# Batch 0's decay rows by a selecting matmul, and copies to q and k that write neighbouring tokens

## The chip, the cores and the metric

The kernel runs on one core of a Trainium2 chip. The metric is the device time of one execution in microseconds, median of the runs. Five engines work side by side, each through its own list of instructions in a fixed order: TensorE (PE; its weight loads are shown apart as PEld), VectorE (DVE), ScalarE (ACT), GpSimd (POOL) and SyncE (SP, which here only issues DMAs).

## The reference

Forgetting attention (causal, with a decay per token), then a gated feed-forward block over all tokens. Batch 8, 8 heads, 576 tokens, head size 64; 4608 tokens of width 512, inner width 1536; everything is given in float32.

```python
scores = scale * np.matmul(q, k.transpose(0, 1, 3, 2))
log_f = np.log(np.clip(f, 0.0001, 1.0))
cum = np.cumsum(log_f, axis=-1)
decay = cum[:, :, :, None] - cum[:, :, None, :]
scores = np.where(causal, -1000000000.0, scores + decay)
attn = softmax(scores)                      # over the last axis
x = np.matmul(attn, v)                      # heads put side by side: (4608, 512)
g = x @ w_gate
out = (g * sigmoid(g) * (x @ w_val)) @ w_out
```

## The kernel before

**Layout.** Scores are taken with the head's 64 values on the partitions. The tile QK holds, for a pair of heads, q and k turned that way, and below them on partitions 64 to 67 four rows for the decay. On q's side these are the cumulated sum times 8 and three rows of ones; on k's side a row of ones and the sum times -8, split into three bf16 parts (high, middle, low). So one matmul over 68 partitions (L581) gives scores and decay. ACT takes the exponential to PT or PTa (L589), POOL masks the diagonal blocks (L598), PE multiplies by v with a column of ones (L612), DVE divides (L619, L626, L628), PE turns the result (L636), and a copy puts it in xT, from where the feed-forward reads.

**Feed-forward.** Per tile of tokens twelve blocks of the inner width: four matmuls with w_gate and four with w_val (L713), tanh on ACT (L717), two operations on DVE (L721, L725). Then w_out (L729), a copy on ACT (L733) and a store on SP (L736). The first 576 tokens, batch 0, are cut into tiles of 256 and 320.

**How q and k come to QK.** Batches 2 to 7: POOL casts them to a bf16 tensor in DRAM (`narrow`), and SP issues transposing loads from there (L452), with the decay rows from DRAM (L455). Batches 0 and 1 don't go that way. Their q and k are loaded as they lie, several neighbouring tokens to a partition (2 in batch 0's first 256 tokens, 4 in its last 320, 6 in batch 1), cast to bf16 in BF, turned by PE (`turn`, L419) with two of the tokens of a partition, 64 values each, on the 128 output partitions, and copied by ACT or DVE (L296, L298) from PSUM to QK. Since a turn leaves tokens of the same place in their partition side by side, the copies (`straighten`, `straighten_a`, `straighten_b`) read PSUM in order and write every sixth, second or fourth token of QK:

```python
dst = QK[:D, hqk[p].i, x::2, :S].rearrange("p j (c u t) -> p j u c t", u=QT // 2, t=2)[:, :, :, :, u]
src = ps(bt).bitcast(BF16)[u * D : (u + 1) * D, :S].rearrange("p (j u c) -> p j u c", j=2, u=QT // 2)
copy(e, dst, src)
```

**Decay rows.** f is loaded with its 64 heads on partitions 0 to 63 and worked in two parts of the tokens (256, then 320): clip, ln, scan, up, high, rest, middle, low (L341 to L364), into `dec`. SP then issues DMAs that put the rows of batch 0 in QK (`row`, L367: four for the first part, four for the second), those of batch 1 (four more) and those of the other batches in DRAM (L392).

**Order.** The kernel writes its instructions by a plan of its own. Each operation has a cost per engine, the operations that it follows, buffers that it takes and a key; `Plan.run` goes through time by these costs and gives each engine the ready operation with the smallest key. The program's order on each engine is fixed by that. Constants steer it: `ready` times for loads (W_AT, WO_AT, Q1_AT, V1_AT), PACE0 and PACE for the transposing loads of batches 2 to 7, TWARM for the time until which PE is taken at half speed, and up to IDLE_TO PE gets dummy matmuls (L819) where it has nothing. PSUM has eight banks: four in pool "f", two in "s", one in "o", one in "t"; early on other work may take banks of "f" and "s".

The functions that the change touches, and what calls them, with their line numbers:

Of the kernel before, what the change touches and what calls it, by code (L numbers as in the profile page):

```python
# [189 lines left out]
PACE, PACE0 = 8.92, 50.3  # L190
# [3 lines left out]
def kernel(ctx, tc, q, k, v, f, w_gate, w_val, w_out, out):  # L194
# [54 lines left out]
    lf, zero, cum, r1 = [HHA[:BH, 2 * i : 2 * i + 2].rearrange("p a s -> p (a s)").bitcast(F32) for i in range(4)]  # L249
    dec = HHA[:BH, 8:16].rearrange("p (r w) s -> p r w s", w=2)  # L250
# [15 lines left out]
    TWARM = 20.0  # L266
# [41 lines left out]

    def ld_f(e):
        nc.scalar.dma_start(out=lf, in_=f.rearrange("b h s -> (b h) s"))  # L310

    o_f = op(("ACT", 0.5), ld_f, key=-9, dma=0.6)
    o_zero = op(("POOL", 0.5), lambda e: nc.gpsimd.memset(zero, 0.0), key=-9)
    o_id = op(("POOL", 0.8), lambda e: make_identity(nc, ident[:, :]), key=-8)
# [19 lines left out]
    o_dec = [op(("DVE", 0.5), blank, "dec", key=-7), op(("DVE", 1.5), blank, "dec1", key=-7)]  # L334
# [5 lines left out]
    def clip(e, a, z):  # L340
        nc.vector.tensor_scalar(out=lf[:, a:z], in0=lf[:, a:z], scalar1=1e-4, scalar2=1.0, op0=ALU.max, op1=ALU.min)  # L341

    def ln(e, a, z):
        nc.scalar.activation(lf[:, a:z], lf[:, a:z], AF.Ln)

    def scan(e, a, z):
        nc.vector.tensor_tensor_scan(out=cum[:, a:z], data0=lf[:, a:z], data1=zero[:, a:z],
                                     initial=cum[:, a - 1 : a] if a else 0.0, op0=ALU.add, op1=ALU.add)

    def up(e, a, z):  # L350
        nc.scalar.activation(dec[:, 0, 0, a:z], cum[:, a:z], AF.Copy, scale=8.0)

    def high(e, a, z):
        nc.vector.tensor_scalar_mul(dec[:, 1, 1, a:z], cum[:, a:z], -8.0)

    def rest(e, a, z):
        nc.vector.scalar_tensor_tensor(out=r1[:, a:z], in0=cum[:, a:z], scalar=-8.0, in1=dec[:, 1, 1, a:z],
                                       op0=ALU.mult, op1=ALU.subtract)

    def middle(e, a, z):  # L360
        nc.vector.tensor_copy(dec[:, 2, 1, a:z], r1[:, a:z])

    def low(e, a, z):
        nc.vector.tensor_sub(dec[:, 3, 1, a:z], r1[:, a:z], dec[:, 2, 1, a:z])  # L364
# [7 lines left out]
    gates, o_row, prior = [], [], []  # L372
    for k0, a, z in ((-9, 0, HALF), (5, HALF, S)):
        n = z - a
        c = op(("DVE", dve(n, False)), clip, a, z, after=[o_f], key=k0, tag="clip")
        c = op(("ACT", act(n)), ln, a, z, after=[c], key=k0, tag="ln")
        c = op(("DVE", 0.1 + n / 480), scan, a, z, after=[c, o_zero] + prior, key=k0, tag="scan")
        prior = [c]
        u = op(("ACT", act(n)), up, a, z, after=[c], key=k0, tag="up")
        g = op(("DVE", dve(n, False)), high, a, z, after=[c], key=k0, tag="high")  # L380
        x = op(("DVE", dve(n, False)), rest, a, z, after=[g], key=k0, tag="rest")
        m = op(("DVE", dve(n, False)), middle, a, z, after=[x], key=k0, tag="middle")
        x = op(("DVE", dve(n, False)), low, a, z, after=[m], key=k0, tag="low")
        four = ((0, [u, o_dec[0]]), (1, [g, o_dec[1]]), (2, [m, o_dec[1]]), (3, [x, o_dec[1]]))
        o_row.append([op(("SP", SPi), row, r, 0, a, z, after=w, key=k0 if k0 > 0 else -4.5, dma=0.05 + n / 640, pkt=40.0, tag=("row", r))
                      for r, w in four])
        gates += [u, g, m, x]
    o_row1 = [op(("SP", SPi), row, r, 1, 0, S, after=gates + o_dec, key=95, dma=0.9, pkt=60.0, tag=("row1", r)) for r in range(4)]
    o_warm = op(("ACT", 1.4), lambda e: nc.scalar.activation(warm, cum[:1, :1], AF.Exp), after=gates, key=-9)
# [7 lines left out]
    gone = [o_decd] + o_row[0] + o_row[1] + o_row1  # L397
# [18 lines left out]
    def turn(e, bb, bt, m, w, blocks):  # L416
        t = ps(bt).bitcast(BF16)
        for n in range(blocks):
            nc.tensor.transpose(t[:, n * m : n * m + w], BF[bb.i][: P if w == P else m, n * P : (n + 1) * P],  # L419
                                ident if w == P else ident[:m, :w])  # L420

    def straighten(e, p, x, u, bt):
        dst = QK[:D, hqk[p].i, x::2, :S].rearrange("p j (c u t) -> p j u c t", u=QT // 2, t=2)[:, :, :, :, u]
        src = ps(bt).bitcast(BF16)[u * D : (u + 1) * D, :S].rearrange("p (j u c) -> p j u c", j=2, u=QT // 2)
        copy(e, dst, src)

    def pair_of(g, x):
        i = hqk[2 * g].i
        assert hqk[2 * g + 1].i == i + 1
        return QK[:D, i : i + 2].rearrange("p s (j w) t -> p (s j) w t", w=2)[:, :, x]  # L430

    def straighten_a(e, g, x, u, bt):
        dst = pair_of(g, x)[:, :, :HALF].rearrange("p h (c t) -> p h c t", t=2)[:, :, :, u]
        src = ps(bt).bitcast(BF16)[u * D : (u + 1) * D, : 4 * P].rearrange("p (h c) -> p h c", h=4)
        copy(e, dst, src)

    def straighten_b(e, g, x, u, bt):
        dst = pair_of(g, x)[:, :, HALF:S].rearrange("p h (c u t) -> p h u c t", u=TB // 2, t=2)[:, :, :, :, u]
        src = ps(bt).bitcast(BF16)[u * D : (u + 1) * D, : 8 * PB].rearrange("p (h u c) -> p h u c", h=4, u=TB // 2)
        copy(e, dst, src)  # L440
# [53 lines left out]

    def first_queries(g, key_a, key_b):
        ps2 = (2 * g, 2 * g + 1)
        took = []
        for part, kk0, ld, st, m, w, blocks, n, cost in (
            ("a", key_a, ld_a, straighten_a, P, P, 4, 4 * P, {"ACT": 0.55, "DVE": 0.66}),
            ("b", key_b, ld_b, straighten_b, PB, PB, 8, 8 * P, {"ACT": 0.66, "DVE": 0.8}),  # L500
        ):
            ready = []
            for x, nm in enumerate("qk"):
                kk = kk0 + 0.1 * x + 0.2 * g
                bn = Buf("nata") if part == "a" else Buf("natb", "natw")
                bb, bt = Buf("bf"), Buf("t", ("f", 30.0), ("s", 30.0))
                o1 = op(("SP", SPi), ld, g, nm, bn, take=[bn], key=kk, dma=1.2 if part == "a" else 1.4, pkt=40.0 if part == "a" else 70.0,
                        tag=("ld" + part, g, x), ready=0.0 if part == "a" else 6.5)
                o2 = op({"DVE": n / 1700 + 0.12, "ACT": act(n)}, cast_n,
# [3 lines left out]
                o3 = op(("PE", mm(*[P] * blocks)), turn, bb, bt, m, w, blocks, after=[o2, o_id], take=[bt], use=[bb], key=kk,  # L513
                        tag=("turn" + part, g, x))
                for u in range(2):
                    first = not took
                    o4 = op(cost, st, g, x, u, bt, after=[o3] + ([took[0]] if took else []),
                            take=[hqk[p] for p in ps2] if first else [], use=[bt] if first else [bt] + [hqk[p] for p in ps2],
                            key=kk, tag=("str" + part, g, x, u))
                    if first:  # L520
                        took.append(o4)
# [338 lines left out]
```

## Time and profile before

| | |
|---|---|
| median of 3 runs | 460.34 us (457.36 to 464.15) |
| the profiled execution | 460.65 us, its span 458.9 us |
| PE busy | 407.6 us, 89% of the span |
| PE weight loads | 234.5 us, 51% |
| DVE / ACT / POOL busy | 237.9 / 237.8 / 125.6 us |
| moved by DMA | 50.09 MB, 109 GB/s over the span |
| mean granted PE clock | 0.94 |

Busy times are those of instructions on the engine; an engine can be busy and still not be what the end waits for. The chain that ended last is followed back from the last instruction, each step to what released it. In it PE has 74% of the span, DMA 7%, ACT 7%, DVE 5%, and the issuing on SP 4%. Lines are those of the kernel before.

### The profile page before, as it was taken

How to read it: one execution, taken by the hardware profiler on the slowest of the kernel's cores; microseconds unless marked ns; L12 is line 12 of the kernel's file. 1: busy time of each engine (PE TensorE's matmuls, PEld its weight loads, DVE VectorE, ACT ScalarE, POOL GpSimd, SP SyncE). 2: the span in 40 equal slices, each digit the busy share in tenths (PEclk: the TensorE clock that was granted, in tenths of full speed). 3: DMA queues.
4: the chain of work that ended last, by engine and by line, in shares of the span. 5: the costliest groups of instructions: out<-in, count | busy, mean ns of one | idle time of the engine just before them, and what ended most of it. 6: DMA issues, size and time to landing. Idle time of an engine off the chain costs nothing.

```text
span 458.9 us, 8374 instructions
## 1 busy us (share of the span) xinstructions
PE 407.6 (89%) x3121; PEld 234.5 (51%) x3121; DVE 237.9 (52%) x438; ACT 237.8 (52%) x445; POOL 125.6 (27%) x353
## 2 busy tenths in 40 slices
PE   5769379777999389999979999799999999999996
PEld 3556357544455146655545565356654444444542
DVE  6583557544376114775245735563477184382660
ACT  3858666774357247764755565356662332332331
POOL 9457216013115116434333243223320000000000
PEclk9978759898999869999997999989999999999999
DMA  9999990009777968599799587964400200101102
GB/s 186 191 160 239 200 219 9 0 25 176 129 153 133 75 137 213 109 183 141 174 193 142 88 124 103 206 107 102 87 1 2 91 1 24 69 1 46 47 0 81
DMA packets 112648, 50.09 MB, mean 109 GB/s; under 512 B 97312, under 2 KB 107360, under 8 KB 112224
## 3 DMA queue, kind: packets, MB, share of 16 engines
q1 hardware_dynamic: 97824, 36.44, 40.3%
q0 software_dynamic: 14704, 12.98, 21.1%
q8 instruction: 24, 0.39, 0.4%
q10 hardware_dynamic: 80, 0.15, 0.1%
q14 instruction: 16, 0.13, 0.1%
HBM read 38.34 MB, written 16.96 MB: 120 GB/s over the span
## 4 chain that ended last, share of the span: by engine, by line
PE 74%; DMA 7%; ACT 7%; DVE 5%; SPq 4%; issue 1%; POOL 0%; ACTq 0%; DVEq 0%
PE ps L713 35%; PE ps L729 20%; PE ps L581 9%; PE ps L612 6%; ACT QK L296 5%; DVE QK L298 3%; DMA natv<-in_v_dram 3%; SPq L452 3%; DMA QK<-dec_d 2%; PE ps L636 2%; PE ps L419 1%; DMA QK<-hh 1%; DMA hh<-in_f_dram 1%; ACT PT L589 1%; SPq L461 1%
## 5 line engine op out<-in xcount | busy, mean ns | idle before, releaser
L713 PE MATMUL ps<-xT,wv 128*128 128x512 bf16 (+3 forms) x480 | 117.0, 368 | 1.6 <-DVE QK L298 1.6
L713 PE MATMUL ps<-xT,wg 128*128 128x512 bf16 (+3 forms) x480 | 116.9, 367 | 0.0
L589 ACT ACTIVATE PT<-ps 128x512 bf16<-128x512 f32 (+2 forms) x192 | 91.8, 518 | 43.6 <-PE ps L581 35.1
L721 DVE SCALAR_TENSOR_TENSOR th<-th,ps 128x512 f32<-128x512 f32 (+3 forms) x120 | 75.7, 631 | 68.7 <-ACT th L717 68.3
L729 PE MATMUL ps<-wo,hh 128*128 128x512 bf16 (+1 forms) x444 | 108.3, 385 | 0.0
L717 ACT ACTIVATE th<-ps 128x512 f32<-128x512 f32 (+3 forms) x120 | 67.1, 561 | 76.7 <-PE ps L713 74.5
L581 PE MATMUL ps<-QK 68*128 68x320 bf16 (+4 forms) x448 | 78.4, 277 | 17.0 <-DMA QK<-dec_d 13.2
L725 DVE TENSOR_TENSOR hh<-th,ps 128x512 bf16<-128x512 f32 (+3 forms) x120 | 76.1, 634 | 15.0 <-PE ps L713 3.8
L598 POOL TENSOR_SCALAR_AFFINE_SELECT PT<-PT 128x128 bf16<-128x128 bf16 (+1 forms) x192 | 52.2, 274 | 107.0 <-ACT PT L589 101.3
L713 PEld LDWEIGHTS <-wv 128*128 128x128 bf16 x480 | 47.2, 100 | 41.2 <-issue 2.9
L713 PEld LDWEIGHTS <-wg 128*128 128x128 bf16 x480 | 47.0, 101 | 40.5 <-issue 1.7
L729 PEld LDWEIGHTS <-hh 128*128 128x128 bf16 (+1 forms) x444 | 42.5, 100 | 42.6 <-issue 2.5
L581 PEld LDWEIGHTS <-QK 68*128 68x128 bf16 x448 | 38.2, 103 | 35.3 <-DMA QK<-dec_d 9.9
L619 DVE RECIPROCAL rc<-ps 128x5 f32<-128x5 f32 (+2 forms) x64 | 12.3, 193 | 79.8 <-PE ps L612 79.6
L598 POOL TENSOR_SCALAR_AFFINE_SELECT PTa<-PTa 128x256 bf16<-128x256 bf16 x64 | 26.1, 412 | 92.6 <-ACT PTa L589 90.7
L612 PE MATMUL ps<-VB,PT 128*128 128x65 bf16 x768 | 45.5, 198 | 3.6 <-POOL PT L598 3.6
L733 ACT ACTIVATE ot<-ps 128x512 f32<-128x512 f32 (+1 forms) x37 | 22.1, 597 | 49.4 <-PE ps L729 48.3
L589 ACT ACTIVATE PTa<-ps 128x384 bf16<-128x384 f32 x64 | 30.8, 493 | 28.7 <-PE ps L581 28.4
L612 PEld LDWEIGHTS <-PT 128*128 128x128 bf16 x768 | 37.9, 101 | 14.5 <-POOL PT L598 4.9
L296 ACT ACTIVATE QK<-ps 64x576 bf16<-64x576 bf16 (+2 forms) x19 | 31.4, 1652 | 12.4 <-PE ps L419 9.1
L298 DVE COPY QK<-ps 64x640 bf16<-64x640 bf16 (+2 forms) x13 | 20.4, 1570 | 17.4 <-ACT QK L296 16.6
L626 DVE TENSOR_TENSOR xn<-ps,rc 128x320 bf16<-128x320 f32 x56 | 27.5, 491 | 1.9
(48 smaller groups left out, 190.2 us busy)
## 6 DMA issues: line engine op xcount, KB each, us to landing
out_dram<-ot SPq DMA_DIRECT2D x35, 256.0 KB
natv<-in_v_dram SPq DMA_DIRECT2D x24, 256.0 KB
qk_d<-in_q_dram POOLq DMA_DIRECT2D x6, 576.0 KB, 7.6
qk_d<-in_k_dram POOLq DMA_DIRECT2D x6, 576.0 KB, 11.1
wg<-in_moe_w_gate_dram POOLq DMA_DIRECT2D x3, 512.0 KB, 6.8
wv<-in_moe_w_val_dram POOLq DMA_DIRECT2D x3, 512.0 KB, 10.2
wo<-in_moe_w_out_dram POOLq DMA_DIRECT2D x3, 512.0 KB, 22.9
QK<-qk_d SPq DMA_TRANSPOSE x96
```

Source lines behind the costliest of these rows:

```text
L296: nc.scalar.activation(dst, src, AF.Copy)
L298: E[e].tensor_copy(dst, src)
L581: nc.tensor.matmul(s[:, c : c + w], QK[:KR, hqk[p].i, 2 * j + 1, kt * P : (kt + 1) * P], QK[:KR, hqk[p].i, 2 * j, q0 : q0 + w], start=True ...
L589: nc.scalar.activation(place(h, i)[:, OFFS[i] : OFFS[i] + c], ps(bs)[:, :c], AF.Exp, scale=0.125)
L598: nc.gpsimd.affine_select(out=d, in_=d, pattern=pat, compare_op=ALU.is_ge, fill=0.0, base=0, channel_multiplier=-1,)
L612: nc.tensor.matmul(o[:, lo : lo + D + 1], pt[:, c : c + P], VB[hvb[b].i][:, kt, hb, : D + 1], start=first and n == 0, stop=last and n == l ...
L626: nc.vector.tensor_mul(XN[bx.i][:, qb : qb + nq, j], o, r)
L713: nc.tensor.matmul(ps(bf)[:, :n], w[:, ko, fc * P : (fc + 1) * P], xT[:, ko, t0 : t0 + n], start=(ko == 0), stop=(ko == KD - 1))
L717: nc.scalar.activation(TH[bt.i][:, :n], ps(bf)[:, :n], AF.Tanh, scale=0.5)
L721: nc.vector.scalar_tensor_tensor(out=t, in0=t, scalar=1.0, in1=ps(bf)[:, :n], op0=ALU.add, op1=ALU.mult)
L725: nc.vector.tensor_mul(HH[bh.i][:, lo : lo + n], TH[bt.i][:, :n], ps(bf)[:, :n])
L729: nc.tensor.matmul(ps(bf)[:m, :DM], HH[hs[fc].i][:, lo : lo + m], wo[:, fc, :], start=(fc == 0), stop=(fc == KF - 1))
```

## The change

It has two parts, and the constants of the plan are changed with them.

**Batch 0.** The turn is done head by head (`turn1`, in place of `turn`). The values of one head in BF are the stationary side and the identity the moving side of an ordinary matmul, so the result is float32. Ahead of it a matmul with the selector `sel` writes the whole block of 68 partitions: from 32 prepared rows (`zrow`; four kinds for each of batch 0's eight heads) it picks the head's four onto partitions 64 to 67. One copy (`straighten1`) then takes values and decay rows to QK, for q and k together in the first 256 tokens, one by one in the last 320. It writes neighbouring tokens and reads PSUM in steps. The eight DMAs of `row` for batch 0 go. To prepare `zrow`, batch 0's f is loaded once more, repeated over partitions 0 to 63, and f of all heads now lies on partitions 64 to 127; clip and ln run on both, the scan and five DVE operations (`part0` to `part4`, with masks from POOL as scalars) on the 32 rows in two parts of the tokens. The old chain (scan, up, high, rest, middle, low) runs later, over all tokens at once, for batches 1 to 7.

**Batch 1.** The cast puts the tokens of one head side by side in BF (`cast_t`), so that the turn has the two heads on its output partitions, and the copy of one head (`straighten`) writes neighbours and reads PSUM in steps of 96 elements. There are still sixteen copies of 64x576.

The core of the diff:

```diff
-PACE, PACE0 = 8.92, 50.3
+PACE, PACE0 = 8.64, 54.1
-    TWARM = 20.0
+    TWARM = 3.0
...
+    def ld_f0(e):
+        src = f.rearrange("b h s -> (b h) s")
+        nc.scalar.dma_start(out=lf[: P - BH], in_=src[:H].unsqueeze(0).to_broadcast([(P - BH) // H, H, S]))
     def ld_f(e):
-        nc.scalar.dma_start(out=lf, in_=f.rearrange("b h s -> (b h) s"))
+        nc.scalar.dma_start(out=lf[HI], in_=f.rearrange("b h s -> (b h) s"))
...
+    def selector(e):
+        nc.gpsimd.memset(sel, 0.0)
+        nc.gpsimd.affine_select(
+            out=sel, in_=sel, pattern=[[-1, H], [-H, KR]], compare_op=ALU.not_equal, fill=1.0,
+            base=H * D, channel_multiplier=1,
+        )
...
+    def part0(e, a, z):
+        nc.vector.tensor_scalar(out=zrow[0][:, a:z], in0=cum[LOW, a:z], scalar1=MS[:, 0:1], scalar2=MS[:, 1:2],
+                                op0=ALU.mult, op1=ALU.add)
... (part1 to part4 likewise)
-        o_row.append([op(("SP", SPi), row, r, 0, a, z, after=w, key=k0 if k0 > 0 else -4.5, dma=0.05 + n / 640, pkt=40.0, tag=("row", r))
-                      for r, w in four])
...
+    def cast_t(e, src, bb):
+        copy(e, BF[bb.i][:QP, : QT * P].rearrange("p (t h d) -> p h t d", h=2, d=D), src().rearrange("p h (t d) -> p h t d", d=D))
...
-    def straighten(e, p, x, u, bt):
-        dst = QK[:D, hqk[p].i, x::2, :S].rearrange("p j (c u t) -> p j u c t", u=QT // 2, t=2)[:, :, :, :, u]
-        src = ps(bt).bitcast(BF16)[u * D : (u + 1) * D, :S].rearrange("p (j u c) -> p j u c", j=2, u=QT // 2)
+    def straighten(e, p, x, a, bt):
+        dst = QK[:D, hqk[p].i, 2 * a + x, :S].rearrange("p (c n) -> p c n", n=QT)
+        src = ps(bt).bitcast(BF16)[a * D : (a + 1) * D, :S].rearrange("p (n c) -> p c n", n=QT)
         copy(e, dst, src)
...
+    def turn1(e, h4, xs, bbs, bt, m, nt, lo, h):
+        t, w = ps(bt), m * nt
+        for i, x in enumerate(xs):
+            nc.tensor.matmul(t[:KR, i * w : (i + 1) * w], sel[:, h], zrow[x][:, lo : lo + w].rearrange("p (c t) -> p t c", t=nt),
+                             start=True, stop=True)
+            for n in range(nt):
+                nc.tensor.matmul(t[:D, i * w + n * m : i * w + (n + 1) * m],
+                                 BF[bbs[i].i][:m, (h4 * nt + n) * D : (h4 * nt + n + 1) * D], ident[:m, :m], start=True, stop=True)
+
+    def straighten1(e, h, xs, bt, m, nt, lo):
+        w, j = m * nt, h % 2
+        dst = QK[:KR, hqk[h // 2].i, 2 * j + xs[0] : 2 * j + xs[-1] + 1, lo : lo + w].rearrange("p x (c t) -> p x c t", t=nt)
+        src = ps(bt)[:KR, : len(xs) * w].rearrange("p (x t c) -> p x c t", x=len(xs), t=nt)
         copy(e, dst, src)
...
-    for p in range(FB):
-        attention(p, (100 * p, 1000 + 100 * p), PARTS[0])
+    for p in range(FB):
+        attention(p, (1.2 + 0.6 * p, 1000 + 100 * p), PARTS[0])
...
-W_AT = [0.0, 18.9, 19.0]
-WO_AT = [18.1, 19.0, 22.1]
+W_AT = [0, 9.7, 22.2]
+WO_AT = [26.9, 28.3, 32.3]
-V1_AT = 0.9
+V1_AT = 0
```

In the order that follows from it, SP issues batch 0's eight loads first; then, behind the chain of the other batches' rows, the rows of batch 1, the rows for DRAM, six loads of batch 1, five of v, and the last two of batch 1. The first transposing load stands behind two stores; before, it stood behind one.

## The prediction

> **What bounds the kernel now.** I read the forty slices first, then the chain that ended last, then the groups by shape, then the queue that feeds it.
>
> ```profile
> PE   5769379777999389999979999799999999999996
> DMA  9999990009777968599799587964400200101102
> ```
>
> One digit is 11.5 us. TensorE (PE) is short of full work mainly in the first nine slices. DMA is full for six slices, then rests for three (69 to 103 us), though 24 pairs of heads still have to be fetched. That rest is the odd thing in this profile.
>
> ```profile
> 58.66 2.10 DVE QK L298
> 60.80 0.81 PE ps L419 x6
> 61.63 2.09 ACT QK L296
> 63.75 2.08 DVE QK L298
> 65.87 0.48 PE ps L636 x3
> ```
>
> This is the chain of waits (start, length, what). One copy from PSUM to QK follows the other, on ACT or DVE, with a turn of six matmuls between. PE waits for them: one PSUM bank ("t") holds all these turns.
>
> ```profile
> L296 ACT ACTIVATE QK<-ps 64x576 bf16<-64x576 bf16 x11 | 23.0, 2086 | 6.5 <-PE ps L419 5.6 <-PE ps L612 0.6
> L298 DVE COPY QK<-ps 64x576 bf16<-64x576 bf16 x5 | 10.4, 2074 | 12.5 <-ACT QK L296 12.5
> L298 DVE COPY QK<-ps 64x640 bf16<-64x640 bf16 x5 | 7.9, 1579 | 4.5 <-ACT QK L296 4.1 <-PE ps L419 0.3
> L296 ACT ACTIVATE QK<-ps 64x512 bf16<-64x512 bf16 x5 | 3.7, 735 | 2.7 <-DVE QK L298 2.4 <-PE ps L419 0.3
> L298 DVE COPY xT<-ps 128x576 bf16<-128x576 bf16 x28 | 12.7, 454 | 16.8 <-PE ps L636 16.8
> ```
>
> Groups by shape (busy, mean ns | idle before). The 576-wide copy to QK takes 2.08 us on either engine, the 576-wide copy to xT 0.45. All of them read PSUM in unbroken runs; they differ in where they write. `straighten_a` writes every second token (4 bytes apart): 735/512 = 1.4 ns per element. `straighten_b` writes every fourth (8 bytes): 1585/640 = 2.5. `straighten` writes every sixth (12 bytes): 2080/576 = 3.6. The xT copy writes neighbours: 0.8. Two engines of different speed take the same time, so the write limits them.
>
> ```profile
> 55.80 1.28 SPq L405 DMA_DIRECT2D xT<-in_q_dram  x1
> 57.18 0.82 SPq L405 DMA_DIRECT2D xT<-in_k_dram  x1
> 101.31 0.37 SPq L736 DMA_DIRECT2D out_dram<-ot  x1
> 101.78 3.88 SPq L452 DMA_TRANSPOSE QK<-qk_d  x3
> ```
>
> The timeline of SP's queue: after batch 1's last load its next instruction is the first store, which waits until 101.3 for the first output tile. Every transposing load of batches 2 to 7 stands behind that store. So the time of the first output tile sets when the long middle starts.
>
> ```profile
> 46.60:69.00 22.40, 12.79 (x102) 9.46 (x100) 12.81 (x19) 14.43 (x17) 4.87 (x13) 0.62 1.29 210
> 69.00:101.30 32.30, 26.68 (x228) 18.92 (x226) 20.17 (x42) 23.31 (x37) 8.27 (x20) 0.95 0.01 3
> 101.30:131.50 30.20, 27.65 (x221) 14.93 (x220) 14.35 (x27) 12.41 (x22) 5.21 (x15) 0.94 0.78 147
> 345.00:458.90 113.90, 109.53 (x523) 50.78 (x521) 55.79 (x85) 33.37 (x57) 0.00 (x0) 1.00 0.10 36
> ```
>
> Stretches (length; busy PE, PEld, DVE, ACT, POOL; clock; DMA). From 46.6 to 69 PE is busy 12.8 of 22.4 us, at a granted clock of 0.62. The last 114 us are feed-forward alone, PE full: nothing there changes, it only moves.
>
> **The change, part by part.** All sums are against the profiled execution, 460.65 us (span 458.9 and 1.75 around it); the median of the runs is 460.34, so nothing has to be rescaled.
>
> (1) *Batch 1's sixteen copies.* They now write neighbours and read PSUM in steps of 192 bytes. What such a read costs no row shows. Low end: the engines' own pace. ACT's exponentials of 384 and 512 columns take 487 and 603 ns, 0.91 ns per element, so 576 cost 0.66; DVE's L626 reads 320 floats in 0.49 and L628 reads 384 in 0.56, 1.05 ns each, so 0.76. High end: the strided write read backwards. Cost grew 1.1 ns per 4 bytes of step, so from 16 bytes on 4.7 ns per element, 2.7 us a copy. The one strided read in the trace, L619's reciprocals of 4, 5 and 6 elements 260 bytes apart (178, 194, 193 ns), is too short to decide: two more elements cost 15 ns. I take 0.70. The write side, which made the difference between four shapes, becomes that of the xT row, and that row is nearest in width and place. Fourteen of the sixteen lie on the chain (46.64, 48.74, 51.40, 53.59, 56.54, 58.66, 61.63, 63.75, 86.40, 89.06, 91.18, 98.57, 101.66, 103.67): 14 x (2.08 - 0.70) = 19.3 us. The cover below holds: from 46.6 to the first output copy at 100.7, 54 us, PE has 29 us of matmuls at its full pace (four of 256 columns 0.434, of 320 0.544, of 512 0.86), and ACT and DVE, less their copies, about 17 and 27. So PE becomes the bound there, with room for 19 us.
>
> [...]
>
> (2) *PE's clock.* Between 56 and 69 us and around 91 a group of four 256-column matmuls takes 0.85 us instead of 0.434, after waits of 3.4 to 3.7 us for copies. About 12 such groups lose 5 us; with waits under 1.5 us I count half, 2.5.
>
> (3) *Batch 0, first halves.* Eight copies of 64x512 become eight of 68x2x256 floats, one per head for q and k (0.58 to 0.66 at engine pace). The eight row DMAs of L367, on the chain from 10.88 to 16.1, go. In their place: f again, spread over 64 partitions, for 32 rows; five DVE operations instead of four (0.3 to 0.5 each, 0.92 beside POOL's memsets); per head two matmuls of `sel` and four turning ones, 1024 columns, 0.85 us at the half pace that PE shows until 30 us, so 6.8 for eight heads. All heads' turns stand before the first score. The decay rows are ready at about 9.4 (f lands at 4.84 as before, the logarithm's table of 1.28 us is loaded meanwhile, clip, scan and five parts follow), so the first score starts at about 16, or 13 with PE at full pace, against 16.1. I count nothing, bounds -3 to +3. POOL makes masks and selector first: some 13 small instructions of 0.1 to 0.3, so the first v and weight loads go out about 2 us later; the copies of part (4) hide it.
>
> (4) *Batch 0, second halves.* Eight copies of 1.59 become sixteen of 68x320 (0.38 to 0.46). SP no longer sits in the rows from 13.7 to 26.0, so these loads go out at 3 us instead of 11.6. Before, the copies were done at 34 and the 24 exponentials ended at 46.2; ACT was their bound. In the new order ACT has, from about 16: eight exponentials of 0.49, thirteen copies, five of xT, 24 exponentials (12.4), the moved `up` (0.6) and tanh: about 28 us, so 44. Gain 2, bounds -4 to +5. The chain for the other batches' rows (scan, high, rest, middle, low, now 576 wide, some 4.2 us of DVE) moves behind the first attention. Behind `low` wait on SP the row stores and all loads of batch 1; in the order they come six at once, where before the fifth went out at 45.6 only.
>
> (5) *Extra PE work* (some 50 more matmuls) is 3 us at full pace, in stretches where PE waits anyway; without that cover it costs 3.
>
> Sum: 19.3 + 2.5 + 0 + 2 = 23.8 us. First output copy at about 78 instead of 100.7, the middle and the tail moved by as much: 460.65 - 23.8 = 436.9.
>
> **What is late next.** The first transposing load, on SP, now behind the second store and not the first; and batch 2's v and q, k, for which PE already waits between 131 and 163.
>
> **The rivals.**
>
> *A. The gain is halved by the read.* If the strided read costs what a write 8 bytes apart costs (2.48 ns): 14 x (2.08 - 1.43) = 9; batch 0's copies, 9216 elements over two engines, 11.4 us instead of 9.3, so -2; clock and order 3: 450.6. For it: every broken run in this trace costs something. Against: the rows vary only on the write side.
>
> *B. The queues eat it.* DMA is full until 69, so if batch 1's loads, now behind row stores and `low`, come 8 us later, and the first transposing load waits another 8 for the second store (in the old run the second store went 9.2 us after the first), the middle starts at 78 + 16 = 94 instead of 101.8: 452.8. For it: the middle's waits are for v, rows and transposes. Against: the same bytes were through at 69, nine before I need the queue.
>
> *C. Slower: the read costs more than the write did.* At 4.7 ns per element batch 1's copies take 2.7 us, 14 x 0.62 = 8.7 more; batch 0's 24 copies take 21.7 us per engine instead of 9.3, 12.4 more; 2 come back: 480. The point from which it decides: 14 copies of 0.576 us and 4.6 us of batch 0 make 12.7 us for each ns per element, so from the 24 us won at about 1.2 ns nothing is left at 3.1 ns.
>
> **Numbers.** Forecast 0.60, its own range 428 to 448 (part 2 by 2.5 either way, part 3 by 3, part 4 from -3 to +6 against what I took); A 0.14, B 0.14, C 0.12. The range 425 to 457 leaves out C and a little below. Two per cent, about what a measurement of this kernel can tell from no change, is 9.2 us: faster means below 451.1. All of the forecast, half of A and a quarter of B are there: 0.71. The rest of A and B, within two per cent: 0.17. C: 0.12.
>
> **What would show it.** Right: 64x576 copies to QK of 0.6 to 0.8 us; PE waits under 1.5 us between 45 and 78; the first store near 78; DMA's rest shorter than 15 us; the last stretch of 114 us as it is. Wrong: copies above 1.4 us (A or C), or short copies and a first transposing load after 90 (B); first scores after 19 us would break part 3.

## The result, and the profile after

| | before | after |
|---|---|---|
| median | 462.25 us (457.36 to 464.46, 4 runs) | 441.83 us (440.21 to 445.77, 4 runs) |
| the profiled execution (span) | 460.65 us (458.9) | 440.21 us (438.5) |
| mean granted PE clock | 0.94 | 0.93 |
| first scores | 16.1 us | 22.9 us |
| first store | 101.3 us | 90.0 us |
| from the first store to the end of the span | 357.6 us | 348.5 us |

The ratio is 0.9605, with a 95% interval of 0.948 to 0.973. The change is faster by about 4%, as forecast, and the time is 4.9 us above the forecast of 436.9. Medians are over all runs of a kernel, ratios over undisturbed ones only, so a ratio isn't exactly the quotient of two medians.

The forty slices after, one digit for 11 us:

```profile
PE   4899999999789599999988999999999999999995
...
PEclk8555599999999979999996999999999999999999
DMA  8939899239896988797797679646101101102002
```

PE is now nearly full from the second slice on. But from the second to the fifth slice, 11 to 55 us, its clock is at half. "Busy" and "fast" have come apart: the digits of PE look better than before in just the stretch where the kernel now loses time. DMA's rest, three slices before, is now two slices at two and three tenths, and there is a new slice of three tenths from 22 to 33 us.

The groups by shape, the copies to QK (busy, mean ns | idle before, and what ended it):

```profile
L302 ACT ACTIVATE QK<-ps 64x576 bf16<-64x576 bf16 x10 | 6.4, 644 | 2.8 <-PE ps L475 2.2 <-DVE QK L304 0.6
L304 DVE COPY QK<-ps 64x576 bf16<-64x576 bf16 x6 | 4.5, 758 | 0.8 <-PE ps L475 0.7
L302 ACT ACTIVATE QK<-ps 68x320 bf16<-68x320 f32 x12 | 5.2, 430 | 5.9 <-PE ps L488 5.8
```

Batch 1's copies went from 2.08 us to 0.64 on ACT and 0.76 on DVE, and they hardly wait for each other any more: what ends most of their waits is the turn.

The windows of 9.5 to 23 us, 23 to 57 us, 57 to 90 us and the last stretch (length; busy PE, PEld, DVE, ACT, POOL; clock; DMA):

```profile
9.50:23.00 13.50, 11.26 (x49) 4.92 (x49) 9.49 (x17) 5.11 (x9) 3.08 (x17) 0.50 1.28 168
23.00:57.00 34.00, 34.00 (x261) 22.54 (x261) 12.35 (x29) 21.22 (x52) 18.98 (x47) 0.51 0.89 140
57.00:90.00 33.00, 32.93 (x316) 25.59 (x315) 26.20 (x57) 23.36 (x55) 17.17 (x37) 1.00 0.87 153
325.00:438.50 113.50, 108.36 (x507) 50.21 (x513) 55.14 (x84) 32.98 (x57) 0.00 (x0) 1.00 0.10 37
```

In the second row PE is busy for 34.00 of 34 us at a clock of 0.51. In the third it is as busy, at 1.00. Batch 0's second halves are bound by a PE at half pace; batch 1 is bound by PE at full pace; the tail is as it was.

PE's timeline at the start of batch 0 (start, length, what, idle time before it and what ended it):

```profile
9.48 0.37 PE L485 MATMUL ps<-hh 32*68 32x256 bf16 x1 [3.34 <-DVE hh L381]
...
12.44 0.37 PE L485 MATMUL ps<-hh 32*68 32x256 bf16 x1 [2.24 <-DVE hh L396]
...
13.09 0.42 PE L485 MATMUL ps<-hh 32*68 32x256 bf16 x1
13.44 0.42 PE L488 MATMUL ps<-ident,BF 128*64 128x128 bf16 x2
...
22.90 0.82 PE L644 MATMUL ps<-QK 68*128 68x256 bf16 x4
```

L485 is the selecting matmul (32 rows by 68 columns of the array, 256 moving columns), L488 the two turning ones (128 rows by 64 columns, 128 moving each). Each step of 256 moving columns takes 0.35 us, start to start. The first scores begin at 22.9.

The end of the stretch at half pace:

```profile
44.46 0.48 PE L488 MATMUL ps<-ident,BF 80*64 80x80 bf16 x4
...
52.95 1.04 PE L776 MATMUL ps<-xT,wg 128*128 128x256 bf16 x4
...
56.73 0.60 PE L776 MATMUL ps<-xT,wv 128*128 128x256 bf16 x4
```

The last turn of batch 0 starts at 44.5. Behind it come score, value and gate matmuls and turns of the result, in the shapes of the kernel before, and they too run at half pace until 56.2 (four gate matmuls take 0.84 us, start to start, at 53.0, and 0.44 at 56.7); PE isn't idle in between.

SP's queue:

```profile
42.43 3.24 SPq L416 DMA_DIRECT2D QK<-hh  x4
...
89.96 4.10 SPq L799 DMA_DIRECT2D out_dram<-ot  x2
94.16 5.75 SPq L507 DMA_TRANSPOSE QK<-qk_d  x4
```

The row stores, and batch 1's loads behind them, go out from 42.4 on; the last of the loads is issued by 77.6, so SP rests for 12 us. The first store moved by 11.3 us, the first transposing load by 7.6.

### The profile page after: what moved, and what is told of

It is laid out like the page before. It is cut to its first block, busy times and chain, and to the rows that moved or that the text cites. A ratio compares the mean times of both kernels' runs of the same rounds, so it can differ in the third digit from the quotient of the medians.

```text
span 438.5 us, 8459 instructions
## 1 busy us (share of the span) xinstructions
PE 412.1 (94%) x3127; PEld 237.2 (54%) x3173; DVE 230.2 (52%) x440; ACT 221.6 (51%) x458; POOL 128.4 (29%) x366
## 3 DMA queue, kind: packets, MB, share of 16 engines
q0 software_dynamic: 14704, 12.98, 20.9%
## 4 chain that ended last, share of the span: by engine, by line
PE 89%; DMA 6%; DVE 1%; issue 1%; SPq 1%; ACT 0%; POOL 0%; ACTq 0%; DVEq 0%
PE ps L776 40%; PE ps L792 22%; PE ps L644 11%; PE ps L675 7%; DMA natv<-in_v_dram 4%; PE ps L488 3%; PE ps L485 3%; PE ps L699 2%; DMA hh<-in_f_dram 1%; DMA QK<-dec_d 1%; PE ps L475 1%; SPq L507 0%; ACTq L317 0%; POOL VB L304 0%; DVE hh L385 0%
## 5 line engine op out<-in xcount | busy, mean ns | idle before, releaser
L776 PE MATMUL ps<-xT,wg 128*128 128x512 bf16 (+3 forms) x467 | 112.3, 361 | 0.7
L776 PE MATMUL ps<-xT,wv 128*128 128x512 bf16 (+3 forms) x466 | 111.8, 360 | 0.6
L792 PE MATMUL ps<-wo,hh 128*128 128x512 bf16 (+1 forms) x425 | 104.7, 384 | 1.0
L644 PE MATMUL ps<-QK 68*128 68x320 bf16 (+4 forms) x448 | 79.3, 281 | 7.8 <-DMA QK<-dec_d 7.7
L776 PEld LDWEIGHTS <-wv 128*128 128x128 bf16 x480 | 46.1, 98 | 38.5 <-issue 0.9
L776 PEld LDWEIGHTS <-wg 128*128 128x128 bf16 x480 | 45.5, 98 | 37.8 <-issue 0.5
L792 PEld LDWEIGHTS <-hh 128*128 128x128 bf16 (+1 forms) x444 | 42.0, 99 | 41.4 <-issue 1.9
L675 PE MATMUL ps<-VB,PT 128*128 128x65 bf16 x768 | 47.7, 200 | 4.0 <-POOL PT L661 4.0
L675 PEld LDWEIGHTS <-PT 128*128 128x128 bf16 x768 | 40.1, 102 | 16.9 <-POOL PT L661 4.9
L304 DVE COPY xT<-ps 128x576 bf16<-128x576 bf16 (+1 forms) x30 | 13.4, 445 | 21.0 <-PE ps L699 20.9
L302 ACT ACTIVATE QK<-ps 68x320 bf16<-68x320 f32 (+2 forms) x27 | 14.4, 539 | 13.3 <-PE ps L488 10.4
## 6 DMA issues: line engine op xcount, KB each, us to landing
wo<-in_moe_w_out_dram POOLq DMA_DIRECT2D x3, 512.0 KB, 11.3
```

Source lines behind the costliest of these rows:

```text
L302: nc.scalar.activation(dst, src, AF.Copy)
L644: nc.tensor.matmul(s[:, c : c + w], QK[:KR, hqk[p].i, 2 * j + 1, kt * P : (kt + 1) * P], QK[:KR, hqk[p].i, 2 * j, q0 : q0 + w], start=True ...
L675: nc.tensor.matmul(o[:, lo : lo + D + 1], pt[:, c : c + P], VB[hvb[b].i][:, kt, hb, : D + 1], start=first and n == 0, stop=last and n == l ...
L776: nc.tensor.matmul(ps(bf)[:, :n], w[:, ko, fc * P : (fc + 1) * P], xT[:, ko, t0 : t0 + n], start=(ko == 0), stop=(ko == KD - 1))
L792: nc.tensor.matmul(ps(bf)[:m, :DM], HH[hs[fc].i][:, lo : lo + m], wo[:, fc, :], start=(fc == 0), stop=(fc == KF - 1))
```

## The experiments

Two things had to be explained: what made the 20 us, and why the first store is 12 us later than forecast though the copies came out about as priced (batch 0's on ACT at 0.59 and 0.43 us, on DVE at 0.68 and 0.49). The first theory was that batch 1's copies alone make the gain, and that batch 0's new part costs some of it. The rival was that the gain is in the new order of loads and in the constants of the plan. Ratios are to the kernel before on the same chip.

**Batch 1's part alone.** The kernel before, with `cast_t` and the copies that write neighbours, and the constants and the order of before:

```diff
-        dst = QK[:D, hqk[p].i, x::2, :S].rearrange("p j (c u t) -> p j u c t", u=QT // 2, t=2)[:, :, :, :, u]
...
+        dst = QK[:D, hqk[p].i, 2 * a + x, :S].rearrange("p (c n) -> p c n", n=QT)
...
```

> The kernel before with batch 1's part alone: cast_t and the copies that write neighbours. Constants, costs and so the order of every engine are those of before. Theory 1 (batch 1's copies made the gain, and batch 0's part gave some of it back, since its second half ended later than before): 14 copies on the chain x 1.4 us and some of PE's clock, so 20 to 28 us off, 432 to 441 us, faster than the whole change or level with it; first store near 80. Theory 2 (the new order in the middle made about half of the gain): 448 to 454 us. In both the copies take 0.64 us on ACT and 0.76 on DVE.

Measured: 434.9 us, ratio 0.950 (0.942 to 0.959). Its queue and its windows:

```profile
80.37 0.37 SPq L739 DMA_DIRECT2D out_dram<-ot  x1
```

```profile
9.50:23.00 13.50, 8.91 (x67) 6.40 (x64) 7.75 (x13) 9.89 (x17) 6.92 (x15) 1.00 1.35 189
23.00:57.00 34.00, 26.52 (x305) 20.86 (x306) 23.16 (x49) 24.42 (x52) 20.75 (x50) 1.00 1.24 198
```

The first store is at 80.4, 20.9 us earlier than before. In the two windows PE is less busy than in the changed kernel, and in the second it gets through more matmuls (305 records against 261). So this half of the change alone gives as much as the whole, if not more.

The clock of 1.00 in these rows isn't the pace of the first 31 us. Two lines of the same trace show it:

```profile
8.05 1.92 PE L822 MATMUL ps<-ident 128*128 128x256 bf16 x8
...
31.52 0.60 PE L716 MATMUL ps<-xT,wg 128*128 128x256 bf16 x4
```

Eight dummies of 256 columns take 1.92 us, as at half pace; in the run without a selector, below, sixteen take 1.91. From 31.5 on four matmuls of 256 columns take 0.44, start to start. The kernel before, too, reads 1.00 until 24 us, while its dummies up to 21 us come every 0.21 us. So up to the first scores the half pace of the changed kernel is nothing new; what is new is that it lasts without a break to 56 us.

**Batch 1's part undone.** The changed kernel with all of batch 0's part, its order and constants, and batch 1's cast and copies as before (the diff above backwards).

> The changed kernel with batch 1's cast and copies as before (strided writes of 2.08 us); constants, costs and order are those of the change. Theory 1: sixteen copies 1.4 us longer, of which about twelve end up on the chain: 16 to 22 us lost, 456 to 463 us, no better than before. Theory 2: 446 to 452 us, since the copies lie beside full PE work in the new order.

Measured: 458.8 us, ratio 0.999 (0.994 to 1.005).

```profile
L302 ACT ACTIVATE QK<-ps 64x576 bf16<-64x576 bf16 x10 | 20.9, 2090 | 8.0 <-PE ps L475 6.2 <-DVE rc L682 1.8
```

The copies are back at 2.09 us, and nothing of the gain is left. In the profiled execution, of 461.8 us, the first store is at 104.0.

**The constants alone.**

```diff
-PACE, PACE0 = 8.92, 50.3
+PACE, PACE0 = 8.64, 54.1
...
-W_AT = [0.0, 18.9, 19.0]
-WO_AT = [18.1, 19.0, 22.1]
+W_AT = [0, 9.7, 22.2]
+WO_AT = [26.9, 28.3, 32.3]
...
-V1_AT = 0.9
+V1_AT = 0
```

> The kernel before with the change's constants alone (PACE, PACE0, W_AT, WO_AT, V1_AT), nothing else. Theory 1: the copies are still slow, the first store still near 100: 455 to 467 us, within what the order makes of it. Theory 2: 450 to 456 us, by fewer waits of PE for rows of the decay and v after 110 us.

Measured: 464.2 us, ratio 1.012 (0.999 to 1.025). There is no gain in them. With the two runs above, the rival is out: the write stride of sixteen copies made the gain.

**Batch 0's two waits filled.** PE falls to half pace with the waits of 3.34 and 2.24 us (its clock is 0.95 over the first 9.5 us, and 0.50 from there to 23). Dummies ahead of head 0's selecting matmuls take the waits away. In this kernel they overwrite head 0's q in the first 256 tokens, which is lost.

```diff
+            for _ in range((34, 22)[x] if m == P and h == 0 else 0):
+                nc.tensor.matmul(t[:, :HALF], ident, ident.unsqueeze(1).to_broadcast([P, 2, P]), start=True, stop=True)
```

> The changed kernel with 34 dummy matmuls of 256 columns ahead of head 0's first selecting matmul for q and 22 ahead of the one for k, in which PE waits for the decay rows (3.3 and 2.2 us). If PE's half pace from 9.5 to 57 us comes from these two waits and, once released, full pace is held by the small matmuls, batch 0's stage of 47 us loses 8 to 15 us and the kernel is at 426 to 434 us. If the small matmuls (32 to 80 rows, 64 to 68 columns of the array) do not hold it, the stage is the same length, the granted clock there still 0.5, and the time 438 to 444 us.

Measured: 435.1 us, ratio 0.953 (0.944 to 0.963). PE kept full pace until 18.3 us (a clock of 1.00 from 9.5 to 18), and then lost it without any wait; it was at half until about 49 (0.50 from 23 to 45). The first scores came at 21.5, the first store at 85.7. So in the changed kernel the waits start the half pace, but without them it comes all the same, 9 us later: something else ends the full pace too, and keeps it from coming back.

**The change, and batch 1's part alone, once more on one chip**, to have their distance from each other. Neither has an edit.

> The changed kernel as it is, to stand beside the next three on the same chip: 0.955 to 0.965 of the kernel before.

> Batch 1's part alone, as in the first experiment. If batch 0's part and the new constants give time back, this kernel is faster than the changed one on the same chip: a ratio of 0.945 to 0.955 against 0.955 to 0.965. If the difference of the first experiment was scatter between chips, the two are level within 0.5%.

Measured: the change 440.0 us (433.5 to 443.5), ratio 0.954 (0.944 to 0.964), first store 87.4; batch 1's part alone 432.4 us (430.9 to 436.8), ratio 0.946 (0.940 to 0.951), first store 80.8. Batch 0's new part, with its order and constants, costs 6.6 us in the first store. In the time the two ratios are 0.008 apart, some 4 us; the first run of this part and the result, on two chips, are 0.010 apart. Both point the same way, but the intervals overlap, so a loss in time is likely and not shown.

**A matmul over the whole array in every few.** The waits filled, and ahead of each further selecting matmul of batch 0 one dummy of 256 columns over 128 by 128. That makes one matmul in four in the first halves and one in six in the second.

```diff
+            for _ in range((34, 22)[x] if m == P and h == 0 else 1):
+                nc.tensor.matmul(t[:, i * w : i * w + HALF], ident, ident.unsqueeze(1).to_broadcast([P, 2, P]), start=True, stop=True)
```

> The changed kernel with the two waits of PE filled by dummies (34 and 22) and one dummy matmul of 256 columns over the full 128 x 128 array ahead of every head's selecting matmul, 31 more, 3.3 us of PE work at full pace. If PE is held at half pace because the small matmuls use too little of the array, and a full one in five is enough, the clock from 12 to 50 us is 1.0, batch 0's stage ends near 45 instead of 53, and the time is 428 to 434 us. If a full matmul in five is not enough, the clock stays at 0.5, the dummies cost 6.6 us at half pace, and the time is 443 to 448 us.

Measured: 444.2 us, ratio 0.973 (0.967 to 0.979). Full pace was lost at 18.9 us all the same (a clock of 0.50 from 23 to 45), and the dummies had to be paid for.

**Neighbours without the selecting matmul.** The kernel before with batch 1's part, and the same idea in batch 0's second halves: the cast puts two heads side by side, the old turn over 128 columns stays, and the copies of 64x640 write neighbours. The first halves and the row DMAs are as before.

```diff
-        dst = pair_of(g, x)[:, :, HALF:S].rearrange("p h (c u t) -> p h u c t", u=TB // 2, t=2)[:, :, :, :, u]
...
+        dst = QK[:D, i : i + 2, 2 * u + x, HALF:S].rearrange("p s (c t) -> p s c t", t=TB)
...
+    def cast_b(e, src, bb, m, n):
+        for s in range(2):
+            copy(e, BF[bb.i][:m, s * n // 2 : (s + 1) * n // 2].rearrange("p (t u d) -> p u t d", u=2, d=D),
+                 src()[:, 2 * s : 2 * s + 2].rearrange("p u (t d) -> p u t d", d=D))
```

> The kernel before with batch 1's part, and in batch 0's second half the same without the selecting matmul: the old turn over 128 columns, the rows still by DMA, but the cast sets two heads side by side (two instructions instead of one) and the eight copies of 64x640 write neighbours, 0.7 us instead of 1.59. Six of the eight lay on the chain between 19 and 34 us: 6 x 0.85 less 0.3 for the casts, about 4 us below batch 1's part alone, 428 to 434 us, if exponentials on ACT follow at once. If DMA, which is full until 69 us, or ACT's 24 exponentials hold the stage, level with batch 1's part alone.

Measured: 430.0 us, ratio 0.933 (0.925 to 0.940), first store 76.3 in the profiled execution, of 433.3 us.

```profile
L298 DVE COPY QK<-ps 64x640 bf16<-64x640 bf16 x5 | 4.1, 825 | 2.5 <-ACT QK L296 2.2 <-PE ps L422 0.3
L296 ACT ACTIVATE QK<-ps 64x640 bf16<-64x640 bf16 x3 | 2.1, 697 | 2.5 <-PE ps L422 2.5
```

Copies that took 1.58 us take 0.70 and 0.83. Of the kernels that compute all of the reference this one has the lowest ratio, and its interval lies below that of the change on the same chip.

**Wide turns, and their control.** Is it the 64 columns of the turn that lose the clock? The waits are filled, and each turning matmul takes 128 columns; its second half falls on batch 0's decay rows, which are lost. The control is the run with the waits filled once more, on the same chip.

```diff
...
-                                 BF[bbs[i].i][:m, (h4 * nt + n) * D : (h4 * nt + n + 1) * D], ident[:m, :m], start=True, stop=True)
+                                 BF[bbs[i].i][:m, c : c + P], ident[:m, :m], start=True, stop=True)
```

> The changed kernel with the two waits filled by dummies (as in the run with the gaps filled) and with batch 0's turning matmuls widened: each takes two neighbouring blocks of 64 columns of BF as its stationary side, so that it fills 128 columns of the array instead of 64. The number of matmuls, their moving columns and the copies stay. The second block lands on output partitions 64 to 127, over the decay rows of batch 0, so these are left out of the scores (and the last block of each group of four heads is the one before it). If PE stays at half pace in this stage because the small matmuls fill too few columns: the granted clock from 18 to 45 us is 1.0 or near it instead of 0.62, the turns of batch 0's second halves take 0.4 us per head and tensor instead of 0.8, the gates start at about 44 instead of 50.4, and the time is about 428. If the number of columns doesn't decide (short matmuls, or too few rows, or the gaps between them): full pace is lost at 18 to 19 us as before, and the time is 433 to 440.

> The run with the gaps filled once more, on the same chip as the run with wide turns, as its control (the same edit: head 0's q of the first 256 tokens is lost). If nothing but the width differs between them, this one shows full pace until about 18 us, half pace until about 49, the first store at 85 to 87, and 433 to 440 us.

Measured: wide 437.6 us, ratio 0.959 (0.947 to 0.970); control 434.9 us, ratio 0.953 (0.941 to 0.964). The width of the turn alone changes neither the clock nor, as far as these intervals tell, the time. The window of 18 to 23 us, first with wide turns, then the control:

```profile
18.00:23.00 5.00, 5.00 (x27) 2.57 (x27) 2.94 (x5) 2.29 (x5) 0.22 (x1) 0.50 0.83 95
```

```profile
18.00:23.00 5.00, 5.00 (x24) 2.35 (x25) 2.94 (x5) 1.67 (x3) 0.00 (x0) 0.50 1.01 125
```

While the control still has its full clock, its timeline shows something that the clock doesn't account for:

```profile
14.01 0.30 PE L487 MATMUL ps<-hh 32*68 32x256 bf16 x1
14.24 0.30 PE L490 MATMUL ps<-ident,BF 128*64 128x128 bf16 x2
14.47 0.30 PE L487 MATMUL ps<-hh 32*68 32x256 bf16 x1
```

A step of 256 moving columns takes 0.23 us, start to start. In the feed-forward at full pace four matmuls of 256 take 0.434, so one step should be 0.11.

**No selector.** Wide turns, and a matmul over the whole array in place of each selecting one, with as many moving columns. Batch 0's decay rows are not written at all.

```diff
-            nc.tensor.matmul(t[:KR, i * w : (i + 1) * w], sel[:, h], zrow[x][:, lo : lo + w].rearrange("p (c t) -> p t c", t=nt),
...
+            nc.tensor.matmul(t[:, i * w : i * w + HALF], ident, ident.unsqueeze(1).to_broadcast([P, 2, P]), start=True, stop=True)
...
```

> The run with wide turns, and in place of each selecting matmul (32 rows on 68 columns of the array, 256 or 320 moving columns) a matmul of the identity with itself over the whole array of 128 by 128, with as many moving columns (two instructions, 256 and 64, in the second halves). So batch 0's decay rows aren't written at all; the copies, casts and the order stay. If PE falls back to half pace because the array is filled too little on the average (the selector fills an eighth of it for half of the time): the clock stays 1.0 from 9.5 to 23 us, the first scores start at about 19 instead of 21.7, the stage to 45 us is at 0.8 or more, and the time is 425 to 430. If full pace is lost at 17 to 18 us all the same, the filling of the array isn't the cause, and the time is 433 to 440.

Measured: 426.2 us, ratio 0.929 (0.914 to 0.943). The timeline and the windows, from an execution of 428.5 us:

```profile
14.06 0.27 PE L487 MATMUL ps<-ident 128*128 128x256 bf16 x1
14.17 0.28 PE L492 MATMUL ps<-ident,BF 128*128 128x128 bf16 x2
14.29 0.27 PE L487 MATMUL ps<-ident 128*128 128x256 bf16 x1
```

```profile
18.00:23.00 5.00, 4.23 (x68) 3.41 (x67) 4.30 (x11) 4.78 (x14) 4.26 (x7) 1.00 1.37 143
18.00:45.00 27.00, 24.48 (x318) 20.02 (x317) 17.09 (x39) 21.66 (x56) 23.20 (x50) 0.81 1.13 181
```

In the first window both losses are gone at once: a step takes 0.11 us, and the clock is 1.00. The first scores begin at 17.3. So in this stretch the selector's shape is what costs, not the number of matmuls or columns.

But over the 27 us of the second window the clock is only 0.81. All turns are done, and still:

```profile
31.01 0.59 PE L679 MATMUL ps<-VB,PT 128*128 128x65 bf16 x7 [0.79 <-POOL PT L665]
```

From here to about 41 us PE works at half pace, on score and value matmuls, and it comes out of it when the gates run one after the other (four gate matmuls take 0.84 us, start to start, at 38.4, and 0.44 at 41.4). From 28 to 32 us PE was busy for 2.34 of 4 us, and no single wait was longer than 0.79. So half pace also comes, and stays for 10 us, where no matmul has 32 rows or 64 columns.

**The selecting matmul over the whole array.** The same with nothing left out. The prepared rows lie on 128 partitions with zeros below, the selector has 128 columns per head, and in the first 256 tokens the cast leaves 64 zero columns beside each block, so that the turn covers 128 columns and adds to the selected rows. The second halves keep turns of 80 by 64.

```diff
-            nc.tensor.matmul(t[:KR, i * w : (i + 1) * w], sel[:, h], zrow[x][:, lo : lo + w].rearrange("p (c t) -> p t c", t=nt),
-                             start=True, stop=True)
+            nc.tensor.matmul(t[:, i * w : (i + 1) * w], sel[:, h], zall[x][:, lo : lo + w].rearrange("p (c t) -> p t c", t=nt),
+                             start=True, stop=m < P)
+            if m == P:
+                for n in range(nt):
+                    nc.tensor.matmul(t[:, i * w + n * m : i * w + (n + 1) * m],
+                                     BF[bbs[i].i][:, (h4 * nt + n) * P : (h4 * nt + n + 1) * P], ident, start=False, stop=n == nt - 1)
+                continue
...
```

> The change with its array filled, and nothing left out: the prepared rows lie on all 128 partitions (zeros below row 32) and the selector has 128 columns per head (zeros but for four), so the selecting matmul covers the whole array with the same moving columns; in the first 256 tokens the cast leaves 64 zero columns beside each block of 64, so the turn covers 128 columns too and adds to the selected rows in PSUM. The second halves keep their turns of 80 rows by 64 columns. The two waits are filled by dummies as before. Seven small memsets on DVE come first, the selector on POOL is shorter. If the filling of the array decides the clock, and zeros fill it as well as values: 1.0 from 9.5 to 18 us, first scores at 18 to 19 us, the first store at 76 to 80, and 425 to 431 us. If the second halves' narrow turns lose the clock all the same: full pace to about 20, the first store at 82 to 85, 431 to 436. If it was not the filling: as in the run with the gaps filled, 433 to 440.

Measured: 429.1 us (424.4 to 431.4), ratio 0.952 (0.941 to 0.964), the profiled execution 424.37 us.

```profile
18.00:23.00 5.00, 4.69 (x48) 2.55 (x45) 3.98 (x9) 4.82 (x13) 3.65 (x8) 1.00 1.74 184
23.00:45.00 22.00, 21.41 (x271) 15.13 (x271) 16.92 (x39) 16.34 (x41) 18.19 (x40) 1.00 1.11 181
```

```profile
74.31 0.37 SPq L813 DMA_DIRECT2D out_dram<-ot  x1
```

In the two windows the clock is 1.00, the first scores come at 17.7, the first store at 74.3, where the change had 87.4 and 90.0. The second halves still change shape:

```profile
19.11 0.45 PE L494 MATMUL ps<-ot,ot 128*128 128x320 bf16 x1
19.48 0.33 PE L502 MATMUL ps<-ident,BF 80*64 80x80 bf16 x4
```

320 columns, 0.14 us at full pace, take 0.37 and 0.27 from start to start, and the clock holds. This is the fastest of the four executions, with a mean clock of 0.991; the others have 0.960 to 0.980, so they lose the full clock somewhere. All four lie above the nine executions of the change (0.924 to 0.945), and so do those without a selector (0.968 to 0.980). With wide turns it is 0.942 to 0.945, with the control's edit, over both runs, 0.939 to 0.954, with the dummies between the selecting matmuls 0.936 to 0.940. In the trace the stage is what it was meant to be. In the time that isn't shown: the interval overlaps that of the change (0.944 to 0.964), and the two did not run on one chip.

## Why the prediction was right, and where it was not

**Right: batch 1's copies (1) and the clock behind them (2).** Taken 0.70 us a copy, measured 0.68 over both engines (10.9 us for 16). Terms 1 and 2 together, 21.8 us, met the 20.9 and 20.5 us by which the first store moved when batch 1's part stood alone; how these divide between the two terms isn't shown. In the changed kernel the clock from 57 to 90 us is 1.00, and from 56.2, when the gates run at full pace, to the first store it took 33.8 us; I had 34 (44 to 78). The read in steps of 192 bytes, which no row had priced, cost little: ACT took 0.644 us for 576 elements, 1.12 ns each, against my low end of 0.66. DVE took 0.758, 1.32 ns each, as my low end of 0.76 had it, but not the 0.45 of the xT row, which is unbroken on both sides. My high end, 4.7 ns per element from steps of 16 bytes on, was an estimate that carried the rows for 4, 8 and 12 bytes one step further; no run shows such a cost.

**Wrong: batch 0's first halves (3), counted at nothing with 3 us either way.** The first scores came at 22.9, not at 16, and 19 was my own limit for this part. Two terms were too small.

First, the decay rows were ready at 12.4 and not at 9.4. DVE's timeline:

```profile
7.64 0.63 DVE L371 TENSOR_SCALAR hh<-hh 128x320 f32<-128x320 f32 x1 [1.82 <-DMA hh<-in_f_dram]
8.20 0.67 DVE L377 TENSOR_TENSOR_SCAN hh<-hh 32x256 f32<-32x256 f32 x1
...
9.36 1.10 DVE L385 TENSOR_SCALAR hh<-hh,ms 32x256 bf16<-32x256 f32 x1
...
11.02 0.86 DVE L392 TENSOR_SCALAR hh<-hh,ms 32x256 bf16<-32x256 f32 x1
11.92 0.47 DVE L396 SCALAR_TENSOR_TENSOR hh<-hh,ms 32x256 bf16<-32x256 f32 x1
```

In DVE's order the clip of f's second part (L371, 320 wide) stands ahead of the scan of the first, and waits for the second transfer of f until 7.64; two of the five operations then took 0.86 and 1.10 us. I had followed the chain of data and not the queue it stands in.

Second, the turns took 10.5 us and not 6.8. I had 1024 columns per head at half pace, 0.85 us; it was 1.40, four steps of 0.35. At half pace 256 columns are 0.213 us, so each step takes 0.14 us more than its columns, and at full pace 0.23 less 0.11, 0.12 us more. This gap comes where a matmul of 32 rows by 68 columns follows one of 128 by 64 or by 128, or is followed by it (with the wide turns steps of 0.21 to 0.23 us at full pace, 0.32 to 0.36 at half); it is absent where all are 128 by 128 (steps of 0.11 us). The trace of before has no matmul of 32 rows, and 64 columns only in 24 matmuls of w_out that follow one another, eight at a time, so no row priced it. That a change of shape could have a price I had not weighed; the steps here give 0.12 to 0.14 us for each change between 32 by 68 and 128 by 64.

**Wrong: the second halves (4), +2 counted, and the cover of the extra PE work (5).** The cover was "stretches where PE waits anyway". From 23 to 57 us there was none: PE was busy for 34.00 of 34 us at half pace. The 48 more matmuls are 7680 columns, 3.3 us at full pace as I had it; at half pace they are 6.5, and 32 gaps of 0.14 us add 4.5. I had sums for ACT in this stage, made it the bound at 44 us, and made none for PE. The gates reached their full pace at 56, so this part came 12 us later than forecast, some 7 of it from part 3.

That PE stays at half pace for 43 us in which it is never idle I had not thought of. The runs without a selector and with the filled array don't lose the clock in this way; wide turns alone, or a full matmul in four to six, do. Whether it is lost by the part of the array that is used or by the gaps at each change of shape isn't settled, since filling the array took both away in the first halves. Two readings limit both explanations. In the last run the second halves still change shape and the clock stays at 1.00. And half pace outlives the narrow matmuls: by 11 us in the changed kernel, and in the run without a selector it came 1.5 us after the last turn, of which none was narrow. What keeps PE at half pace on ordinary score and value matmuls stays open.

**Too good by luck: the middle.** The first store was 12 us late, but from there to the end the span was 9.1 us shorter, where I had it moved as it stood. So 436.9 against 441.8 is two errors of opposite sign. The second is no larger than what executions of one kernel differ by: that with the waits filled had 351.7 us from the first store to the end on one chip and 341.8 on another. With batch 1's part alone, in the old order, the stretch was 351.9 and 349.8 us. PE's waits behind the first store for decay rows were 13.2 us before and 7.7 after, but 15.4 and 9.6 in these two, so they don't explain it either. Why it was shorter stays open.

**The rivals.** A and C fell with the length of the copies. B's sign, a first transposing load after 90 us, did appear (94.2). B was right that this load waits for the second store, but that took 4.2 us and not 8; the rest has another cause, for the stores waited for PE, which was busy for 32.93 of the 33 us before them. The forecast of faster needed the copies alone, and these were the part that was well priced.

## What to carry to other kernels

Price a copy by both its sides, and look which of them the groups by shape vary on: here a write that skips elements cost some three times the copy (2.08 us against 0.68), and the cast ahead of it sorted the data for the same price (0.66 us on DVE before, 0.64 after; 0.83 on POOL both times). When work is moved onto PE, don't price it by columns alone: here matmuls that alternate between few rows or columns and the full array left a gap at each change (0.14 us at half pace, for 256 columns of 0.213), and padding with zeros to 128 by 128 took the gap away at no cost in PE time (a step of 0.11 us). Where such matmuls stood, the clock was at half as well (0.50); filling the array raised it (to 1.00), by which of its effects isn't known. Read PE's busy share, its granted clock and the distance of its matmuls together, and for each stage add up the engine that you are about to load, not only the one that was the bound.

## What was not expected of the hardware

- A PE that issued back to back from 12.4 to 56 us stayed at a clock of 0.50, though its last narrow turn started at 44.5; and with the waits filled and a selector of 32 rows PE lost full pace at 16.5 to 18.9 us without a wait. A wait of 3.34 us went with the end of full pace in the changed kernel; 43 us in which PE was always busy did not bring it back.
- The granted clock reads 1.00 early in a trace (to 21 us in the kernel before, to 31 with batch 1's part alone) while matmuls of 256 columns come every 0.21 us, as at half pace.
- Zeros stood in for data: in the filled selector all but 4 of a head's 128 columns are zero, and all but 32 of the rows that it multiplies, and the clock was 1.00 from 18 to 45 us.
- A change between 32 by 68 and 128 by 64 cost 0.12 us at full pace, 0.14 at half; between 32 by 68 and 128 by 128 it was 0.10 to 0.12 us, and 0.11 to 0.15. From 128 by 128 to 80 by 64 and back it was 0.23 and 0.13 us. From 128 by 128 to 80 by 128 no gap shows (640 columns, 0.27 us at full pace, in 0.29).
- Steps of 4, 8 and 12 bytes in the write cost ACT and DVE the same (0.735 and 0.716 us for 512 elements, 1.589 and 1.579 for 640, 2.086 and 2.074 for 576). Steps in the PSUM read cost ACT nothing that shows: 640 elements went from 1.59 to 0.70 us when the step moved from the write to the read. DVE lost only the pace that it has with both sides unbroken (576 elements 0.76 us, against 0.45).
